# Attention and MLP block on one core: the first five units take their softmax denominators through one ones-matmul, the first statistics move partly to ScalarE, and queries run three units ahead

## Chip, cores and metric

One core of a Trainium2 chip. The metric is device microseconds of one execution of the program; lower is better. The kernel before was run three times: 1280.09, 1280.42 and 1280.76 us, so its median is 1280.42 us.

## What is computed

The reference, cut to what matters (`_layernorm` has eps 1e-5, `_B_ref` is an MLP block with two gelu layers on the same normed tokens):

```python
def _A_ref(x, k_cache, v_cache, wq, wo):          # x: 2048 x 512, 32 heads of 128, 2048 keys
    q = (x @ wq).reshape(B, Sq, H, Dh).transpose(0, 2, 1, 3)
    p = softmax(einsum("bhqd,bhkd->bhqk", q, k_cache) * Dh ** -0.5)
    o = einsum("bhqk,bhkd->bhqd", p, v_cache)
    return o.transpose(0, 2, 1, 3).reshape(B, Sq, H * Dh) @ wo

x = A_x
xn = _layernorm(x)
s = _A_ref(xn, A_k_cache, A_v_cache, A_wq, A_wo)
g = silu(_B_ref(xn, B_w1, B_w2, B_w3, B_w4))
return x + s * g
```

All inputs are bf16. The kernel subtracts no maximum in the softmax; the denominator is the sum over keys of exp(scores).

## The kernel before

**Units and slots.** The attention is cut into 128 units. A unit is one head and 512 queries (L121: eight groups of four heads; in a group the four blocks of 512 queries in turn, and in each block its four heads). A unit has eight slots (`SPU`, L54), each for two chunks of 128 keys. The main loop (L695) runs over all 1024 slots n; u is the unit, p the slot in it. In a slot TensorE makes two score matmuls into a two-bank PSUM tile `ps_s` (`s_slot`, L183), ScalarE takes exp of the 128x1024 tile into `pT` (L194), and TensorE makes the two value matmuls of five slots earlier into `ps_o` (`pv_slot`, L213, `LAG`, L55). `ps_s`, `ps_o` have two buffers each, `pT` four (two slots in each), and the two tags of the pool `psX`, "xa" and "xm", one bank each.

**Denominators.** VectorE adds the unit's four `pT` tiles: `add_first` at p = 4 (L200), `add_next` at p = 6 (L205), `add_last` at p = 0 of the next unit (L205, then a fold of 1024 columns, L210, and of 512, L211). That leaves for each query 128 partial sums, one on each partition. `sums` (L223), at p = 3 of the next unit, turns them into sums with four matmuls of one column each; the 512 sums then lie as 128 partitions x 4. `recip` (L231) inverts them (L233) and writes them to DRAM (`dr<-rc`, L235); `bcast` (L248), at p = 4, reads them back to all 128 partitions (`rb<-dr`, L250). `norm` (L253), at p = 2 of the second unit after, multiplies `ps_o` by `rb` into `oT` (L261).

**Queries.** `q_mm` (L167) makes a unit's 512 queries with four matmuls, `q_copy` (L175) casts them to `qT` (L180 on VectorE). Unit 0 has its own start (`first_tokens`, L377). Queries of units 1 to 3 are made in unit 0, those of unit 4 at the end of unit 2, and from unit 3 on those of unit u + 2 at p = 0 and 1 of unit u (L701 to L714).

**Layer norm.** 16 tiles of 128 tokens. A tile is loaded (L343), VectorE takes its statistics (L349, L350), GpSimd makes 1/sqrt(var + eps) of them in two small instructions (`rsqrt`, L116: L118, L119), VectorE applies mean and factor (L354), and the result is turned: for tiles 0 to 3 by TensorE against an identity (L386 to L400), for all others by a DMA transpose on SP's queue into `xnT` (L370). The first four tiles come ahead of the loop (L643 to L658); for the others a list of slots, `tokens` (L661), says when statistics, application and transpose are put into the queues.

**Order.** Every instruction of the path is pinned in program order, so each engine works through the order in which the code issues it, and what is issued after slot n by `at(n, ...)` stands behind that slot's own work in its engine's queue. Keys come by DMA transposes on SP's queue (`load_k`, L141), values by plain DMAs (`load_v`, L150, on SP too); for the heads of the first group their places are L649 to L673. SP's and GpSimd's DMAs pass eight completion semaphores in turn.

**MLP.** Its 136 chunks of four to five matmuls are spread over the slots p = 2, 3, 6 and 7 of units 5 to 119 (L638, L746); the output projections `wo_mm` (L266) fill p = 4 and 5 from unit 5 on. Until unit 5 there is nothing of either.

Of the kernel before, what the change touches and what calls it, by code (L numbers as in the profile page):

```python
# [8 lines left out]
ACT = mybir.ActivationFunctionType  # L9
ALU = mybir.AluOpType  # L10
# [7 lines left out]
def kernel(  # L18
# [40 lines left out]
    SHIFT = [1, -1, 2, -2]  # L59
    PADW = 8  # L60
    WARM = 48
    PSUM = bass.MemoryType.PSUM
    pin = tc.keep_in_program_order

    def pool(name, bufs=1, space=None, **kw):
# [9 lines left out]
    nhalf = const.tile([P, 1], FP32, name="nhalf")  # L75
    mv2 = const.tile([P, NT, nc.vector.BN_AGGR_DIM], FP32, name="mv2")
    rstd2 = const.tile([P, NT], FP32, name="rstd2")
    nc.vector.memset(ones_t[:], 1.0)
    nc.vector.memset(nhalf[:], -0.5)
    ident = const.tile([P, P], BF16, name="ident")  # L80
    diag = const.tile([P, P], FP32, name="diag")
# [1 line left out]
                       allow_small_or_imprecise_dtypes=True))  # L83
    pin(nc.vector.tensor_scalar(
        out=ident[:], in0=diag[:], scalar1=0.0, scalar2=None, op0=ALU.is_equal))

    kp = ent(pool("kp", HG + 1))
    vp = ent(pool("vp", HG + 1))
# [24 lines left out]
    def mm(out, lhsT, rhs, start, stop):  # L113
        pin(nc.tensor.matmul(out=out, lhsT=lhsT, rhs=rhs, start=start, stop=stop))  # L114

    def rsqrt(out, var):  # L116
        ve = smp.tile([P, 1], FP32, name="ve")
        pin(nc.gpsimd.tensor_scalar(out=ve[:], in0=var, scalar1=EPS, scalar2=None, op0=ALU.add))  # L118
        pin(nc.gpsimd.tensor_tensor(out=out, in0=ve[:], in1=nhalf[:], op=ALU.pow))  # L119

    units = [(g, qt, hh) for g in range(NG) for qt in range(QT) for hh in range(HG)]  # L121
    NU = len(units)
# [7 lines left out]
    def at(n, fn):  # L130
        todo[n].append(fn)
# [18 lines left out]
    def load_v(h, halves):  # L150
        v = A_v_cache[0, h].rearrange("(i p j) d -> p i j d", p=P, j=KJ)
        for i in halves:
            if i == 0:
                vBs[h] = vp.tile([P, KC, Dh], BF16, name="vb")
            ks = slice(i * KSPLIT // 2, (i + 1) * KSPLIT // 2)
            pin(nc.sync.dma_start(
                out=vBs[h].rearrange("p (i j) d -> p i j d", j=KJ)[:, ks], in_=v[:, ks]))

    def load_w(h, eng=nc.sync):
# [7 lines left out]
    def q_mm(u, dcs):  # L167
        g, qt, hh = units[u]
        if dcs[0] == 0:
            st[u] = dict(psq=psX.tile([P, 512], FP32, tag="xm" if u == HG else "xa", name="ps_q"))  # L170
        for dc in dcs:
            mm(st[u]["psq"][:], wqs[g * HG + hh][:, dc, :],
               xnT[:, dc, qt * 512:(qt + 1) * 512], dc == 0, dc == DC - 1)

    def q_copy(u):  # L175
        qT = qtp.tile([P, 512], BF16, name="qT")
        if u > QUIET + 1:
            pin(nc.scalar.activation(out=qT[:], in_=st[u].pop("psq")[:], func=ACT.Identity))
        else:
            pin(nc.vector.tensor_copy(out=qT[:], in_=st[u].pop("psq")[:]))  # L180
        st[u]["qT"] = qT
# [31 lines left out]
    def pv_slot(u, p):  # L213
# [5 lines left out]
        for j in range(2):  # L219
            kc = 2 * p + j  # L220
            mm(s["o"][:], vBs[g * HG + hh][:, kc, :], pT[:, 2 * (p % 2) + j, :], kc == 0, kc == KC - 1)

    def sums(u):  # L223
        s = st[u]
        ps = psX.tile([P, 4], FP32, tag="xa" if u + 1 < QUIET else "xm", name="ps_sum")
        a = s["acc"][:, 0, :].rearrange("k (p j) -> k j p", j=4)
        for j in range(4):
            mm(ps[:, j:j + 1], a[:, j, :], ones_t[:], True, True)
        recip(s, ps)

    def recip(s, ps):  # L231
# [5 lines left out]
    def split_sums(u, parts):  # L237
        s = st[u]
        if "ps" not in s:
            s["ps"] = psX.tile([P, 4], FP32, tag="xm", name="ps_sum")  # L240
        for a, first, last in parts:
            a = a.rearrange("k (p j) -> k j p", j=4)
            for j in range(4):
                mm(s["ps"][:, j:j + 1], a[:, j, :], ones_t[:], first and j == 0, last and j == 3)
        if parts[-1][2]:
            recip(s, s["ps"])

# [89 lines left out]


    ln = {}

    def ln1_load(t, eng):
        xin = tokp.tile([P, D], BF16, tag="ta", bufs=8, name="xin")
# [3 lines left out]
    def ln1_stats(t):  # L346
        xin = ln[t]
        bn = smp.tile([P, nc.vector.BN_STATS_DIM], FP32, name="bn")
        pin(nc.vector.bn_stats(out=bn[:], in_=xin[:]))  # L349
        pin(nc.vector.bn_aggr(out=mv1[t][:], in_=bn[:]))  # L350
        rsqrt(rs1[t][:], mv1[t][:, 1:2])

    def norm1(t, out, in_):
        pin(nc.vector.tensor_scalar(  # L354
# [3 lines left out]
    def ln1_norm(t):  # L358
        xin = ln.pop(t)
        xn = tokp.tile([P, D], BF16, tag="tb", bufs=8, name="xn")  # L360
        norm1(t, xn[:], xin[:])
        return xn
# [12 lines left out]
            mm(wt[:, 0, 0:P], ident[:], ident[:], True, True)  # L375

    def first_tokens():  # L377
        xns = [ln1_norm(t) for t in range(4)]
        st[0] = {}
        qA = psX.tile([P, 512], FP32, tag="xa", name="ps_q")  # L380
        qB = psX.tile([P, 512], FP32, tag="xm", name="ps_q")
        qT = qtp.tile([P, 512], BF16, name="qT")
        st[0]["qT"] = qT
        tps = []

        def turn(t):  # L386
            if t < 2:
                tp = psO.tile([P, DC, P], FP32, tag="ps_o", name="ps_o")[:]
            else:
                tp = psS.tile([P, 2, 512], FP32, name="ps_s")[:, 0, :].rearrange("p (c q) -> p c q", c=DC)  # L390
            for dc in range(DC):
                mm(tp[:, dc, :], xns[t][:, dc * P:(dc + 1) * P], ident[:], True, True)
            tps.append(tp)

        def back(t):
            dst = xnT[:, :, t * P:(t + 1) * P]
            if t == 2:
                pin(nc.vector.tensor_copy(out=dst, in_=tps[t]))
            else:
                pin(nc.scalar.activation(out=dst, in_=tps[t], func=ACT.Identity))  # L400

        def q_part(t):
# [12 lines left out]
        pin(nc.vector.tensor_copy(out=qT[:, 3 * P:], in_=qB[:, 3 * P:]))  # L415
# [49 lines left out]
    mv1 = [ph1.tile([P, nc.vector.BN_AGGR_DIM], FP32, name=f"mv1_{t}") for t in range(NT)]  # L465
    rs1 = [ph1.tile([P, 1], FP32, name=f"rs1_{t}") for t in range(NT)]

    def ph1_load():
        pin(nc.sync.dma_start(out=w1_sb[:], in_=B_w1.rearrange("(dc p) j -> p dc j", p=P)))
# [176 lines left out]
    pin(nc.scalar.activation(out=act1[:], in_=nhalf[:], func=ACT.Identity))  # L646
# [6 lines left out]
    for t in range(4):  # L653
        ln1_stats(t)
# [5 lines left out]
    load_k(2, (0, 1))  # L660
    tokens = ((2, 4, 5), (5, 9, 12), (8, 12, 13), (11, 14, 14),  # L661
              (21, 27, 27), (23, 29, 29), (29, 35, 35), (35, 39, 39),
              (39, 45, 45), (47, 53, 53), (55, 61, 61), (63, 69, 69))
    for t, (stats, apply, turn) in enumerate(tokens, 4):
        if t >= 8:
            at(stats - 8, lambda t=t: ln1_load(t, nc.gpsimd))
# [23 lines left out]
    for t in range(4 * LQ, NT):  # L690
        if t % 4 < 2:
            at((QUIET + 1 + 2 * (t % 4)) * SPU + 4, lambda t=t: gate_sum(t))

    wo_todo = deque()
    for n in range(NS):  # L695
        u, p = divmod(n, SPU)
# [1 line left out]
        m = n - LAG  # L698
        if m >= 0:
            pv_slot(*divmod(m, SPU))  # L700
        if u == 0 and p in (1, 3, 5):  # L701
            q_mm(1 + p // 2, range(DC))
        if u == 0 and p in (2, 4, 6):
            q_copy(p // 2)
        if u == HG - 2 and p in (6, 7):
            q_mm(HG, (2 * p - 12, 2 * p - 11))
        if u == HG - 2 and p == 7:
            q_copy(HG)
# [4 lines left out]
        if p == 2 and HG - 1 <= u < NU - 2:  # L713
            q_copy(u + 2)  # L714
        if p == 2 and u >= 2:
            norm(u - 2)
            gg, qq, hh = units[u - 2]
# [121 lines left out]
```

## Time and profile before

| what | value |
|---|---|
| runs | 1280.09, 1280.42, 1280.76 us |
| the profiled execution, its own time | 1279.53 us |
| its span, first to last instruction | 1277.8 us |
| TensorE matmul / ScalarE / VectorE busy | 98% / 87% / 80% |
| granted TensorE clock | 0.999 |
| matmuls, VectorE instructions | 6195, 1407 |
| DMA traffic | 111.79 MB, mean 87 GB/s |

How to read it: the profile is of one execution. A line such as `L205 DVE TENSOR_TENSOR` is the instruction of that line of the program, PE is TensorE, PEld its weight load, DVE VectorE, ACT ScalarE, POOL GpSimd, SP SyncE; a q behind the name is the engine's queue of issues. "<-" is read "made from" in a tile name and "released by" behind an idle time. Matmul rows overlap one another, so a busy TensorE row can be longer than the time that the matmul adds. The timeline gives start and duration of every instruction; the difference between the starts of two neighbours on a busy engine is what the first one costs in the queue.

### The profile page before, as it was taken

The numbers are of one execution on the slowest core, as the hardware profiler recorded it, in microseconds if no ns is written. First come the engines' busy times: TensorE is split into PE (matmuls) and PEld (weight loads), VectorE is DVE, ScalarE is ACT, GpSimd is POOL, SyncE is SP. The second block draws the span as 40 slices with busy tenths as digits, with TensorE's granted clock in tenths as the row PEclk, the third lists the DMA queues.
The fourth block names the chain that finished last, engine by engine and source line by source line (L and its number), as shares of the span: only waits on it lengthen the run. The fifth ranks groups of instructions, "written<-read, shape, count | busy, mean of one in ns | idle before, by whom it ended". The sixth has DMA issues, their size and how long they took to land.

```text
span 1277.8 us, 17233 instructions
## 1 busy us (share of the span) xinstructions
PE 1257.1 (98%) x6195; PEld 612.1 (48%) x6320; DVE 1019.2 (80%) x1407; ACT 1113.0 (87%) x1195; POOL 137.9 (11%) x241
## 2 busy tenths in 40 slices
PE   8999999999999999999999999999999999999998
PEld 5444444444444444444444444444444444444444
DVE  7888889898788877778887778887777888777886
ACT  7899998888999988899988889998888999888883
POOL 4430003323110010000001000000000000000110
PEclk9999999999999999999999999999999999999999
DMA  9644343455532564134443244523435133542532
GB/s 185 133 106 81 59 79 88 108 124 123 115 77 67 100 110 89 42 75 83 89 93 68 58 85 93 96 42 75 96 80 90 34 70 72 91 105 46 140 76 58
DMA packets 172950, 111.79 MB, mean 87 GB/s; under 512 B 124800, under 2 KB 149888, under 8 KB 172864
## 3 DMA queue, kind: packets, MB, share of 16 engines
q1 hardware_dynamic: 163904, 85.51, 34.3%
q0 software_dynamic: 8672, 24.91, 7.9%
q8 instruction: 49, 0.80, 0.3%
q14 instruction: 37, 0.30, 0.1%
q10 hardware_dynamic: 288, 0.26, 0.1%
HBM read 82.58 MB, written 7.60 MB: 71 GB/s over the span
## 4 chain that ended last, share of the span: by engine, by line
PE 87%; ACT 6%; DVE 4%; issue 1%; DMA 1%; POOL 0%; DVEq 0%; ACTq 0%
PE ps_s L114 31%; PE ps_o L114 30%; PE ps_m L114 9%; PE ps_wo L114 8%; PE ps_q L114 7%; ACT pT L194 4%; PE ps_sum L114 1%; ACT sq L425 1%; DVE acc L205 1%; ACT pre L455 1%; DVE bn L349 0%; DMA rb<-dr 0%; DMA xnT<-xn 0%; DVE acc L210 0%; DVE qT L180 0%
## 5 line engine op out<-in xcount | busy, mean ns | idle before, releaser
L194 ACT ACTIVATE pT<-ps_s 128x1024 bf16<-128x1024 f32 x1024 | 1012.0, 1031 | 141.0 <-PE ps_s L114 130.0
L114 PE MATMUL ps_s<-qT,kT 128*128 128x512 bf16 x2004 | 599.5, 379 | 4.1 <-ACT pT L194 1.0
L114 PE MATMUL ps_o<-pT,vb 128*128 128x512 bf16 x1997 | 597.6, 379 | 2.8
L205 DVE TENSOR_TENSOR acc<-acc,pT 128x2048 bf16<-128x2048 bf16 x254 | 309.8, 1220 | 65.5 <-ACT pT L194 60.8
L114 PEld LDWEIGHTS <-kT 128*128 128x128 bf16 x2048 | 226.8, 113 | 224.4 <-issue 18.6
L114 PEld LDWEIGHTS <-vb 128*128 128x128 bf16 x2048 | 199.8, 98 | 225.2
L200 DVE TENSOR_TENSOR acc<-pT 128x2048 bf16<-128x2048 bf16 x128 | 155.9, 1218 | 26.6 <-ACT pT L194 26.4
L114 PE MATMUL ps_q<-xnT,wq_h 128*128 128x512 bf16 (+1 forms) x519 | 150.7, 374 | 3.3 <-DMA xnT<-xn 2.0
L114 PE MATMUL ps_wo<-wo_h,oT 128*128 128x512 bf16 x456 | 136.3, 379 | 0.6
L328 DVE TENSOR_TENSOR s_acc<-ps_wo,s_acc 128x512 f32<-128x512 f32 x100 | 68.9, 689 | 73.9 <-PE ps_wo L114 71.0
L210 DVE TENSOR_TENSOR acc<-acc 128x1024 bf16<-128x1024 bf16 x127 | 87.9, 692 | 4.4
L261 DVE TENSOR_TENSOR oT<-ps_o,rb 128x512 bf16<-128x512 f32 x129 | 87.1, 676 | 4.1 <-DMA rb<-dr 4.0
L180 DVE CAST qT<-ps_q 128x512 bf16<-128x512 f32 x122 | 83.5, 685 | 4.8 <-PE ps_q L114 4.8
L114 PEld LDWEIGHTS <-wq_h 128*128 128x128 bf16 x524 | 50.6, 98 | 63.2 <-issue 3.6
L114 PEld LDWEIGHTS <-oT 128*128 128x128 bf16 x480 | 46.9, 98 | 57.7 <-issue 2.6
L114 PE MATMUL ps_m<-xn2T,w_sb 128*128 128x512 bf16 x222 | 66.1, 378 | 0.2
L114 PE MATMUL ps_m<-w_sb,h2T 128*128 128x512 bf16 x218 | 62.7, 379 | 0.2
L577 POOL DMA_DIRECT2D w_sb<-in_B_w_dram x28 | 21.1, 756 | 353.8 <-PE ps_m L114 328.6
L211 DVE TENSOR_TENSOR acc<-acc 128x512 bf16<-128x512 bf16 x127 | 54.0, 425 | 4.3
L233 DVE RECIPROCAL rc<-ps_sum 128x4 f32<-128x4 f32 x128 | 22.9, 179 | 40.9 <-PE ps_sum L114 40.0
L114 PEld LDWEIGHTS <-acc 128*128 128x128 bf16 x516 | 37.6, 115 | 29.6 <-issue 1.5
L609 POOL DMA_DIRECT2D g_d<-xr x16 | 8.8, 547 | 346.3 <-DVE xr L607 346.3
(74 smaller groups left out, 599.9 us busy)
## 6 DMA issues: line engine op xcount, KB each, us to landing
rb<-dr SPq DMA_DIRECT2D x128, 256.0 KB, 4.1
vb<-in_A_v_cache_dram SPq DMA_DIRECT2D x64, 256.0 KB, 4.5
w_sb<-in_B_w_dram POOLq DMA_DIRECT2D x28, 256.0 KB, 4.6
wo_h<-in_A_wo_dram SPq DMA_DIRECT2D x32, 128.0 KB, 3.9
wq_h<-in_A_wq_dram SPq DMA_DIRECT2D x28, 128.0 KB, 4.2
kT<-in_A_k_cache_dram SPq DMA_TRANSPOSE x128, 4.7
dr<-rc SPq DMA_DIRECT2D x128, 2.0 KB, 1.4
xr<-in_A_x_dram POOLq DMA_DIRECT2D x16, 128.0 KB, 3.5
```

Source lines behind the costliest of these rows:

```text
L114: pin(nc.tensor.matmul(out=out, lhsT=lhsT, rhs=rhs, start=start, stop=stop))
L180: pin(nc.vector.tensor_copy(out=qT[:], in_=st[u].pop("psq")[:]))
L194: pin(nc.scalar.activation(out=s["pT"][-1][:, jj:jj + 2, :], in_=sps[:], func=ACT.Exp, scale=SCALE))
L200: pin(nc.vector.tensor_tensor(out=s["acc"][:], in0=s["pT"][0][:], in1=s["pT"][1][:], op=ALU.add))
L205: pin(nc.vector.tensor_tensor(out=a[:], in0=a[:], in1=st[u]["pT"][i][:], op=ALU.add))
L210: pin(nc.vector.tensor_tensor(out=a[:, 0:2, :], in0=a[:, 0:2, :], in1=a[:, 2:4, :], op=ALU.add))
L211: pin(nc.vector.tensor_tensor(out=a[:, 0, :], in0=a[:, 0, :], in1=a[:, 1, :], op=ALU.add))
L233: pin(nc.vector.reciprocal(out=rc[:], in_=ps[:]))
L261: pin(nc.vector.tensor_tensor(out=oTs[(g, qt)][:, hh, c], in0=s["o"][:, c], in1=s["rb"][:, c], op=ALU.mult))
L328: pin(nc.vector.tensor_tensor(out=sa, in0=ps[:], in1=sa, op=ALU.add))
L425: pin(nc.scalar.activation(out=sq[:], in_=pre[:], func=ACT.Square, scale=GELU_A ** 0.5))
L577: pin(nc.gpsimd.dma_start(out=w[:], in_=w3_v[:, :, fc * P:(fc + 2) * P]))
```

## The change

It touches the first units and what runs ahead of them; from unit 6 on only the lead of the queries differs.

1. **Denominators of units 0 to 4** (`ONCHIP` = 5): `ones_t` becomes 128x128, and `sums_here` makes one matmul of 512 columns with the ones as weights, so each partition gets all 512 sums. VectorE inverts them from PSUM, 128x512, straight into `rb`. The four one-column matmuls, `dr<-rc` and `rb<-dr` of these five units go.
2. **First statistics:** tiles 0 and 2 stay on VectorE; tiles 1 and 3 take two passes of ScalarE each (`Identity` and `Square`, both with an accumulated sum), and a small VectorE instruction makes the mean. GpSimd makes the four factors in three pairs of instructions.
3. **Queries:** from unit 2 on those of unit u + 3 are made in unit u; those of unit 4 at slots 14 and 15 (`first_q`).
4. **Places:** the statistics, applications and transposes of tiles 4 to 7 move from slots 2 to 14 into slots 3 to 8; pieces 1 to 3 of the keys of head 2, until now issued ahead of the loop and at slots 2 and 4, come at slots 9 to 11, those of head 3 at 14 to 17, and the values of heads 2 and 3 go to GpSimd's queue.

```diff
+    ONCHIP = HG + 1
+    QL = 3
-    ones_t = const.tile([P, 1], BF16, name="ones_t")
+    ones_t = const.tile([P, P], BF16, name="ones_t")
...
     def q_mm(u, dcs):
-            st[u] = dict(psq=psX.tile([P, 512], FP32, tag="xm" if u == HG else "xa", name="ps_q"))
+            st[u] = dict(psq=psX.tile([P, 512], FP32, tag="xm" if u >= QUIET + QL else "xa", name="ps_q"))
...
+    def sums_here(u):
+        s = st[u]
+        ps = psX.tile([P, 512], FP32, tag="xm" if u + 1 < ONCHIP else "xa", name="ps_sum")
+        mm(ps[:], ones_t[:], s["acc"][:, 0, :], True, True)
+        s["rb"] = rp.tile([P, 512], FP32, name="rb")
+        pin(nc.vector.reciprocal(out=s["rb"][:], in_=ps[:]))
...
     def sums(u):
-        ps = psX.tile([P, 4], FP32, tag="xa" if u + 1 < QUIET else "xm", name="ps_sum")
+        ps = psX.tile([P, 4], FP32, tag="xa", name="ps_sum")
...
+    def first_stats():
...
+        def act(t):
+            pin(nc.scalar.activation(
+                out=junk[t][:], in_=ln[t][:], func=ACT.Identity, scale=-root / D, accum_out=nm[t][:]))
+            pin(nc.scalar.activation(
+                out=junk[t][:], in_=ln[t][:], func=ACT.Square, scale=root, bias=nm[t][:],
+                accum_out=mvA[:, t, 1:2]))
...
+        dve(0)
+        act(1)
+        dve(2)
+        act(3)
+        root_of(0, 1)
+        root_of(1, 3)
+        root_of(3, 4)
...
-    tokens = ((2, 4, 5), (5, 9, 12), (8, 12, 13), (11, 14, 14),
-              (21, 27, 27), (23, 29, 29), (29, 35, 35), (35, 39, 39),
+    tokens = ((3, 4, 5), (4, 5, 6), (5, 6, 7), (6, 7, 8),
+              (19, 23, 23), (21, 25, 25), (25, 29, 29), (29, 33, 33),
               (39, 45, 45), (47, 53, 53), (55, 61, 61), (63, 69, 69))
...
-    for n, h, piece in ((2, 2, 2), (4, 2, 3), (12, 3, 0), (15, 3, 1), (17, 3, 2), (20, 3, 3)):
+    for n, h, piece in ((9, 2, 1), (10, 2, 2), (11, 2, 3), (14, 3, 0), (15, 3, 1), (16, 3, 2), (17, 3, 3)):
         at(n, lambda h=h, piece=piece: load_k(h, (piece,)))
-    for n, h, half in ((7, 2, 0), (13, 2, 1), (20, 3, 0), (21, 3, 1)):
-        at(n, lambda h=h, half=half: load_v(h, (half,)))
+    for n, h, half in ((10, 2, 0), (11, 2, 1), (20, 3, 0), (22, 3, 1)):
+        at(n, lambda h=h, half=half: load_v(h, (half,), nc.gpsimd))
...
+    first_q = {1: (1, range(DC)), 3: (2, range(DC)), 5: (3, range(DC)),
+               14: (4, (0, 1)), 15: (4, (2, 3))}
+    first_copy = {2: 1, 4: 2, 6: 3, 15: 4}
...
-        if p in (0, 1) and HG - 1 <= u < NU - 2:
-            q_mm(u + 2, (2 * p, 2 * p + 1))
+        if p in (0, 1) and 2 <= u < NU - QL:
+            q_mm(u + QL, (2 * p, 2 * p + 1))
...
-            sums(u - 1)
-        if p == 4 and u >= 1:
+            (sums_here if u - 1 < ONCHIP else sums)(u - 1)
+        if p == 4 and u > ONCHIP:
             bcast(u - 1)
```

The applications of tiles 1 and 3 take their mean from the small VectorE instruction put ahead of them (`mean_of` in `first_tokens`). In VectorE's queue of the changed program, after statistics 4 and the cast of unit 2's queries, the order is: `add_first(0)`, apply 4, statistics 5, apply 5, statistics 6, cast of unit 3's queries, `add_next(0)`, apply 6, statistics 7, apply 7, `add_last(0)`, reciprocal 0.

More of the change, by code (lines that the diff above doesn't have):

```diff
@@ L73 @@
     s_acc = const.tile([P, NT, D], FP32, name="s_acc")
-    ones_t = const.tile([P, 1], BF16, name="ones_t")
-    nhalf = const.tile([P, 1], FP32, name="nhalf")
+    ones_t = const.tile([P, P], BF16, name="ones_t")
+    nhalf = const.tile([P, 2], FP32, name="nhalf")
     mv2 = const.tile([P, NT, nc.vector.BN_AGGR_DIM], FP32, name="mv2")
     rstd2 = const.tile([P, NT], FP32, name="rstd2")
-    nc.vector.memset(ones_t[:], 1.0)
     nc.vector.memset(nhalf[:], -0.5)
@@ L85 @@
         out=ident[:], in0=diag[:], scalar1=0.0, scalar2=None, op0=ALU.is_equal))
+    pin(nc.vector.memset(ones_t[:], 1.0))
     kp = ent(pool("kp", HG + 1))
@@ L118, in rsqrt @@
         pin(nc.gpsimd.tensor_scalar(out=ve[:], in0=var, scalar1=EPS, scalar2=None, op0=ALU.add))
-        pin(nc.gpsimd.tensor_tensor(out=out, in0=ve[:], in1=nhalf[:], op=ALU.pow))
+        pin(nc.gpsimd.tensor_tensor(out=out, in0=ve[:], in1=nhalf[:, 0:1], op=ALU.pow))
     units = [(g, qt, hh) for g in range(NG) for qt in range(QT) for hh in range(HG)]
@@ L148, in load_k, with load_v @@
                 in_=A_k_cache[0, h, i * w:(i + 1) * w, :], transpose=True))
-    def load_v(h, halves):
+    def load_v(h, halves, eng=nc.sync):
         v = A_v_cache[0, h].rearrange("(i p j) d -> p i j d", p=P, j=KJ)
@@ L155, in load_v @@
             ks = slice(i * KSPLIT // 2, (i + 1) * KSPLIT // 2)
-            pin(nc.sync.dma_start(
+            pin(eng.dma_start(
                 out=vBs[h].rearrange("p (i j) d -> p i j d", j=KJ)[:, ks], in_=v[:, ks]))
@@ L176, in q_copy @@
         qT = qtp.tile([P, 512], BF16, name="qT")
-        if u > QUIET + 1:
+        if u >= QUIET + QL:
             pin(nc.scalar.activation(out=qT[:], in_=st[u].pop("psq")[:], func=ACT.Identity))
@@ L221, in pv_slot @@
             mm(s["o"][:], vBs[g * HG + hh][:, kc, :], pT[:, 2 * (p % 2) + j, :], kc == 0, kc == KC - 1)
+    def sums_here(u):
[4 more added lines that the diff above has]
+        pin(nc.vector.reciprocal(out=s["rb"][:], in_=ps[:]))
     def sums(u):
         s = st[u]
[L225 removed]
+        ps = psX.tile([P, 4], FP32, tag="xa", name="ps_sum")
         a = s["acc"][:, 0, :].rearrange("k (p j) -> k j p", j=4)
         for j in range(4):
[L228 removed]
+            mm(ps[:, j:j + 1], a[:, j, :], ones_t[:, 0:1], True, True)
         recip(s, ps)
@@ L243, in split_sums @@
             for j in range(4):
-                mm(s["ps"][:, j:j + 1], a[:, j, :], ones_t[:], first and j == 0, last and j == 3)
+                mm(s["ps"][:, j:j + 1], a[:, j, :], ones_t[:, 0:1], first and j == 0, last and j == 3)
         if parts[-1][2]:
@@ L339 @@
     ln = {}
+    mvA = const.tile([P, 4, nc.vector.BN_AGGR_DIM], FP32, name="mvA")
+    rsA = const.tile([P, 4], FP32, name="rsA")
     def ln1_load(t, eng):
@@ L351, in ln1_stats, with dve, mean, root_of @@
         rsqrt(rs1[t][:], mv1[t][:, 1:2])
+    def first_stats():
+        root = D ** -0.5
+        nm = {t: smp.tile([P, 1], FP32, name="nm") for t in (1, 3)}
+        junk = {t: gtp.tile([P, D], BF16, tag="pre", name="pre") for t in (1, 3)}
+        def act(t):
[4 more added lines that the diff above has]
+                accum_out=mvA[:, t, 1:2]))
+        def dve(t):
+            bn = smp.tile([P, nc.vector.BN_STATS_DIM], FP32, name="bn")
+            pin(nc.vector.bn_stats(out=bn[:], in_=ln[t][:]))
+            pin(nc.vector.bn_aggr(out=mvA[:, t, :], in_=bn[:]))
+        def mean(t):
+            pin(nc.vector.tensor_scalar(
+                out=mvA[:, t, 0:1], in0=nm[t][:], scalar1=-1.0 / root, scalar2=None, op0=ALU.mult))
+        def root_of(a, b):
+            ve = smp.tile([P, b - a], FP32, name="ve")
+            pin(nc.gpsimd.tensor_scalar(
+                out=ve[:], in0=mvA[:, a:b, 1], scalar1=EPS, scalar2=None, op0=ALU.add))
+            pin(nc.gpsimd.tensor_tensor(
+                out=rsA[:, a:b], in0=ve[:], in1=nhalf[:, 0:b - a], op=ALU.pow))
+        dve(0)
[5 more added lines that the diff above has]
+        root_of(3, 4)
+        return mean
     def norm1(t, out, in_):
@@ L377, in first_tokens @@
     def first_tokens():
-        xns = [ln1_norm(t) for t in range(4)]
+        xns = []
+        for t in range(4):
+            if t % 2:
+                mean_of(t)
+            xns.append(ln1_norm(t))
         st[0] = {}
@@ L464 @@
     hT = ph1.tile([P, DC, Sq + PADW], BF16, name="hT")
-    mv1 = [ph1.tile([P, nc.vector.BN_AGGR_DIM], FP32, name=f"mv1_{t}") for t in range(NT)]
-    rs1 = [ph1.tile([P, 1], FP32, name=f"rs1_{t}") for t in range(NT)]
+    mv1 = [mvA[:, t, :] for t in range(4)]
+    mv1 += [ph1.tile([P, nc.vector.BN_AGGR_DIM], FP32, name=f"mv1_{t}") for t in range(4, NT)]
+    rs1 = [rsA[:, t:t + 1] for t in range(4)]
+    rs1 += [ph1.tile([P, 1], FP32, name=f"rs1_{t}") for t in range(4, NT)]
     def ph1_load():
@@ L645 @@
     act1 = const.tile([P, 1], FP32, name="act1")
-    pin(nc.scalar.activation(out=act1[:], in_=nhalf[:], func=ACT.Identity))
+    pin(nc.scalar.activation(out=act1[:], in_=nhalf[:, 0:1], func=ACT.Identity))
     for h in range(HG - 1):
@@ L652 @@
     warm_up(WARM)
-    for t in range(4):
-        ln1_stats(t)
+    mean_of = first_stats()
     load_w(HG - 1, nc.gpsimd)
@@ L659 @@
     load_v(1, (0, 1))
-    load_k(2, (0, 1))
-    tokens = ((2, 4, 5), (5, 9, 12), (8, 12, 13), (11, 14, 14),
-              (21, 27, 27), (23, 29, 29), (29, 35, 35), (35, 39, 39),
+    load_k(2, (0,))
+    tokens = ((3, 4, 5), (4, 5, 6), (5, 6, 7), (6, 7, 8),
+              (19, 23, 23), (21, 25, 25), (25, 29, 29), (29, 33, 33),
               (39, 45, 45), (47, 53, 53), (55, 61, 61), (63, 69, 69))
@@ L665 @@
         if t >= 8:
-            at(stats - 8, lambda t=t: ln1_load(t, nc.gpsimd))
+            at(stats - 6, lambda t=t: ln1_load(t, nc.gpsimd))
         at(stats, lambda t=t: ln1_stats(t))
@@ L700 @@
             pv_slot(*divmod(m, SPU))
[L701 to L708, printed above, removed]
-        if p in (0, 1) and HG - 1 <= u < NU - 2:
-            q_mm(u + 2, (2 * p, 2 * p + 1))
+        if n in first_q:
+            q_mm(*first_q[n])
+        if n in first_copy:
+            q_copy(first_copy[n])
+        if p in (0, 1) and 2 <= u < NU - QL:
+            q_mm(u + QL, (2 * p, 2 * p + 1))
         if p == 0 and u >= 1:
             add_last(u - 1)
-        if p == 2 and HG - 1 <= u < NU - 2:
-            q_copy(u + 2)
+        if p == 2 and 2 <= u < NU - QL:
+            q_copy(u + QL)
         if p == 2 and u >= 2:
```

## Prediction

> **What bounds the kernel now.** I read the page's shares first: TensorE's matmuls fill 98% of the span, and the chain that ended last is 87% TensorE. So for most of the span only fewer matmuls or less idle time would help, and the change takes away neither; it can only move time in the first units. The busy time by stretches of 10 us (columns: stretch, length, then busy us of TensorE, its weight load, VectorE, ScalarE, GpSimd, with counts) shows where TensorE isn't full:
>
> ```profile
> 10.00:20.00 10.00, 9.36 (x41) 4.43 (x43) 7.17 (x12) 8.61 (x10) 2.34 (x6) 1.00 1.19 249
> 20.00:30.00 10.00, 9.95 (x52) 4.86 (x52) 9.38 (x18) 10.00 (x12) 3.69 (x6) 1.00 0.62 132
> 30.00:40.00 10.00, 7.99 (x37) 3.68 (x37) 7.11 (x11) 6.87 (x9) 4.66 (x6) 1.00 0.86 141
> 40.00:50.00 10.00, 9.77 (x52) 4.74 (x52) 9.19 (x17) 9.32 (x11) 2.91 (x12) 1.00 0.79 173
> ...
> 80.00:90.00 10.00, 9.95 (x50) 4.91 (x50) 9.00 (x13) 9.46 (x12) 5.38 (x9) 1.00 0.72 200
> ```
>
> TensorE loses 0.64 us from 10 to 20 and 2.0 from 30 to 40, while VectorE runs at 9.4 and 9.2 of 10: early, VectorE has no room either. TensorE's waits from 30 to 60 us (total, times, longest) name what was lost:
>
> ```profile
> PE ps_q L114 <- DMA xnT<-xn: 2.0, 1, 2.0
> PE ps_sum L114 <- DVE qT L180: 0.6, 2, 0.4
> ```
>
> The first is the transpose of the next tokens: queries of unit 4 waited for `xnT`. The chain of waits in the same time (start, us, what) goes through VectorE's additions and the transfers:
>
> ```profile
> 17.95 1.14 DVE acc L205
> ...
> 19.18 1.24 DVE acc L205
> 20.44 0.70 DVE acc L210
> 21.16 0.43 DVE acc L211
> ...
> 28.84 0.69 DVE oT L261
> 29.54 4.31 DMA xnT<-xn
> ...
> 41.03 2.97 DMA dr<-rc
> 44.01 4.38 DMA rb<-dr
> ```
>
> The end of the fold (21.16 + 0.42) is where `sums` of unit 0 starts; its matmul stands in TensorE's queue, so nothing behind it starts earlier. In the timeline the sums of units 0 to 5 start at 21.78, 29.11, 40.37, 48.35, 57.39 and 67.66 us. I use these six marks: the change has done all it does by the last.
>
> **What a step costs.** Two neighbouring matmuls of 512 columns advance the chain by 0.43 us, so 0.2157 each. VectorE's steps, from start to next start in its timeline: addition of 2048 columns 1.14, or 1.26 if the next one uses its result (27.66 - 26.40); the folds 0.73 and 0.35, so `add_last` 2.34; query cast and `norm` 0.61 each; statistics 0.73 + 0.10; application 0.32. A step is about 0.09 shorter than the row's duration.
>
> **Part 2, the first statistics.** Now all four statistics run on VectorE before the first application (6.62), and GpSimd's fourth factor ends at 7.84, so the last application starts at 7.88. Afterwards ScalarE has tiles 1 and 3. A pass over 512 columns isn't in the trace with an accumulated sum; the row L604 (0.62 us, 512 columns from SBUF) is the nearest. From 3.6 (tile 1 landed, 3.57) four passes end at 6.2, the factor at 7.15, the application at 7.2: 0.7 us earlier. If each accumulation adds 0.2, nothing is won; the bound on the other side is GpSimd's three pairs one after another from 4.41, 0.87 each: 0.85. I take 0.6. The small mean instruction is under 0.2 and lies in GpSimd's time.
>
> **Part 4, the tokens in unit 0.** This is what I expect to cost first. An application right behind its own statistics waits for GpSimd, as the timeline of tile 6 shows:
>
> ```profile
> 22.23 0.18 DVE L350 BATCH_NORM_AGGREGATE mv<-bn 128x2 f32<-128x6 f32 x1
> ...
> 22.50 0.29 POOL L118 TENSOR_SCALAR ve<-mv 128x1 f32<-128x1 f32 x1 [4.16 <-DVE mv L350]
> ...
> 22.87 0.57 POOL L119 TENSOR_TENSOR rs<-ve,nhalf 128x1 f32<-128x1 f32 x1
> ```
>
> From the start of the aggregation to the factor's end it takes 23.44 - 22.23 = 1.2 us, where VectorE's step is 0.1. In the new order applications 5 and 7 stand right behind statistics 5 and 7: two bubbles of 1.1 us. Laid out: cast of unit 2's queries 13.8 (14.40 less 0.6), `add_first(0)` 14.4, application 4 at 15.6, statistics 5 15.9, bubble, application 5 17.8, statistics 6 18.1, cast 18.95, `add_next(0)` 19.55, application 6 20.7, statistics 7 21.0, bubble, application 7 22.9, `add_last(0)` 23.2 to 25.6. So sum 0 starts at **25.7 instead of 21.78**. Queued behind it on TensorE is slot 12, and ScalarE's exp behind that. Roughly, 2.2 of it are the bubbles and 2.6 the steps of tokens 6 and 7 that now stand ahead of the fold, less the 0.6.
>
> **Parts 1 and 3, denominators and queries, unit by unit.** Gone: four one-column matmuls (67.66 to 67.80: 0.14), a 0.09 step of VectorE, five `dr<-rc` and five `rb<-dr`. Their 0.32 to 0.34 us on SP's queue lie beside other work; their landing (2.97 + 4.38 in the chain) gave `norm` one wait of 0.46 us. New: one matmul of 0.22, and **a reciprocal of 128x512 from PSUM**. The trace has it only with four columns (mean ns after the busy time):
>
> ```profile
> L261 DVE TENSOR_TENSOR oT<-ps_o,rb 128x512 bf16<-128x512 f32 x127 | 86.4, 680 | 3.6 <-DMA rb<-dr 3.6
> L180 DVE CAST qT<-ps_q 128x512 bf16<-128x512 f32 x122 | 83.5, 685 | 4.8 <-PE ps_q L114 4.8
> ...
> L233 DVE RECIPROCAL rc<-ps_sum 128x4 f32<-128x4 f32 x128 | 22.9, 179 | 40.9 <-PE ps_sum L114 40.0
> ...
> L261 DVE TENSOR_TENSOR oT<-ps_o,rb 128x256 bf16<-128x256 f32 x2 | 0.8, 418 | 0.5 <-DMA rb<-dr 0.5
> ...
> L415 DVE CAST qT<-ps_q 128x128 bf16<-128x128 f32 x1 | 0.3, 290 | 1.0 <-PE ps_q L114 1.0
> ```
>
> The cast and `norm` give what a PSUM source costs: (685 - 290)/384 = 1.03 ns a column and 158 fixed, and (680 - 418)/256 = 1.02 and 156 fixed. Four columns would then take 160 ns, the reciprocal takes 179. If the 19 to 23 ns more belong to the four columns, one costs 5.2 to 5.8 ns, and 512 cost 2.8 to 3.1 us. If they are fixed, it's 0.69, as the cast; that is the lower bound, since no row of this shape is cheaper. With the longest row (184) and a fixed part of 150, it's 8.5 ns and 4.5 us, the upper. I take 3.1 (step 3.0), since a fixed extra would need a reason that no row gives.
>
> [...]
>
> VectorE between two sums, with the reciprocal behind cast and `norm`:
>
> - 0 to 1: wait for the sum 0.5, reciprocal 3.0, additions 1.26 + 1.14, cast 0.61, last 2.34: 8.86. TensorE needs 41 matmuls, 8.84.
> - 1 to 2: 1.22 + 3.0 + statistics 8, 9 1.66 + additions 2.28 + application 0.32 + 2.34 = 10.83 against 37 matmuls, 7.98.
> - 2 to 3: two applications and two statistics, second addition 1.26: 11.27 against 7.98.
> - 3 to 4: one of each, additions 1.26 + 1.14: 10.12 against 7.98.
> - 4 to 5: `ps_sum` of unit 4 takes the tag "xa", so unit 5's first `wo_mm` waits until the reciprocal is read: 1.22 + 3.0, and then 40 matmuls, 8.63: 12.83 together against 49 matmuls, 10.57.
>
> 25.7 + 8.86 + 10.83 + 11.27 + 10.12 + 12.83 = 79.6, **11.95 us later** than 67.66. ScalarE's exp waits with it: slot 0 of the next unit needs the buffer that `add_first` frees. The stall for `xnT` (2.0) goes, but VectorE is late there in any case. The same queries are made in all, one unit's four earlier, so 0.86 comes back at unit 125: **11.1 us**. After unit 6 nothing else differs. Pieces 1 to 3 of head 2's keys now stand on SP behind the transpose of tile 7 (23.3 + 1.2): the first leaves at 24.5, lands some 4 later (as the `kT` issues of that time do), and slot 18 needs it at about 33, so 4 us of cover; if sum 0 came at 21.2, that cover would be gone. The values on GpSimd's queue leave after the last factor (22.9), land by 29 and are needed at slot 21.
>
> The profiled execution took 1279.53; 1279.53 + 11.1 = 1290.6. The median of the runs is 0.9 above it: **1291.5 us**.
>
> **Rivals.**
> - *Dear reciprocal* (upper end, 4.5): each us of it counts five times, so 7.0 more, **1298.5**. For it: the longest rows. Against: the mean row. [...]
> - *Cheap reciprocal* (0.69, step 0.6): the intervals become 8.84, 8.42, 8.86, 7.98, 10.57, the mark 70.4, 2.7 late, less 0.86: **1282.3**. For it: the 20 ns may be fixed. It decides below about 1.5 us, where TensorE's 43.4 us equal VectorE's.
> - *Transfers, not VectorE, set units 0 to 5*, so the change wins: sum 0 at 21.2 and TensorE's own intervals (8.84, three of 7.98, 10.57) give 64.6, 3.1 early, with the 0.86 4.0: **1276.5**. For it: 29.54 to 33.85 and 41.03 to 48.39 in the chain are DMA. Against: VectorE's 9.4 of 10. It needs sum 0 by 22.4 and a reciprocal under 1.2 us.
>
> **Chances.** Forecast (reciprocal 2 to 3.9, 1286 to 1295.5) 0.62; dear 0.14; cheap 0.13; transfers 0.11. A measurement of this kernel tells about 0.2% (2.6 us) from no change. Faster: 0.11 and 0.02 of the cheap case, 0.13; same: 0.07 of the cheap case; slower: 0.80. The range leaves out the transfers, half of the cheap case's lower part and little of the dear one: **1281 to 1299**.
>
> **What would show it.** A row RECIPROCAL 128x512 of about 3.1 us, five times; `ps_sum` starts near 25.7, 34.6, 45.4, 56.7, 66.8 and 79.6; TensorE waiting some 4 us for `acc` before sum 0; VectorE idle 1 us for GpSimd ahead of applications 5 and 7; VectorE's second 40th of the span full. The forecast is wrong if the reciprocal is under 1.5 us, if sum 0 starts by 22.4, or if time is lost behind unit 6.

## The result and the profile after

| kernel | median (lowest to highest) | ratio to before [95% interval] |
|---|---|---|
| before | 1280.26 us (1280.05 to 1280.76) | |
| after | 1296.42 us (1295.59 to 1297.02) | 1.0125 [1.0108, 1.0143] |

The change costs 16.2 us; 11.1 were forecast. The profiled execution of after took 1297.02 us, 17.49 above that of before. Its groups by line show the new operation beside the old one (after the bar: busy us, mean ns of one):

```profile
L230 DVE RECIPROCAL rb<-ps_sum 128x512 f32<-128x512 f32 x5 | 16.8, 3351 | 1.1 <-PE ps_sum L116 1.1
...
L242 DVE RECIPROCAL rc<-ps_sum 128x4 f32<-128x4 f32 x123 | 22.0, 179 | 41.0 <-PE ps_sum L116 40.2
```

From the two rows a column costs (3351 - 179)/508 = 6.24 ns, with 154 ns fixed: the fixed part is that of the cast and `norm`, and the 20 ns more belong to the columns. Stretches of 10 us, as those shown of before:

```profile
20.00:30.00 10.00, 5.50 (x17) 2.00 (x16) 8.23 (x10) 4.11 (x5) 3.93 (x7) 0.72 0.64 133
30.00:40.00 10.00, 10.00 (x44) 4.60 (x43) 8.63 (x10) 7.96 (x9) 0.00 (x0) 0.93 0.42 77
40.00:50.00 10.00, 7.80 (x35) 3.42 (x33) 9.63 (x16) 6.97 (x8) 5.60 (x10) 1.00 0.45 93
...
70.00:80.00 10.00, 7.22 (x25) 2.95 (x25) 8.40 (x9) 3.77 (x5) 0.76 (x3) 0.83 0.12 27
```

From 40 to 50 VectorE is at 9.63 and TensorE has fallen to 7.80: VectorE bounds these units. The column behind the five engines is the granted clock: 0.72, 0.93 and 0.83 here, where before has 1.00 in these stretches. From 30 to 40 TensorE is "busy" for all of its 10 us, but the first 1.3 of them at half clock. TensorE's waits from 0 to 100 us:

```profile
PE ps_sum L116 <- DVE acc L213: 7.7, 3, 4.5
PE ps_wo L116 <- DVE rb L230: 2.2, 1, 2.2
...
PE ps_sum L116 <- DVE qT L182: 1.6, 1, 1.6
```

The 4.5 us stand ahead of sum 0, the 2.2 are unit 5's `wo_mm` behind the last reciprocal: both as forecast. The wait of before for `xnT` is gone. In VectorE's timeline the two bubbles ahead of applications 5 and 7:

```profile
18.46 0.41 DVE L402 TENSOR_SCALAR xn<-xin,mv,rs 128x512 bf16<-128x512 bf16 x1 [0.99 <-POOL rs L121]
...
23.53 0.41 DVE L402 TENSOR_SCALAR xn<-xin,mv,rs 128x512 bf16<-128x512 bf16 x1 [1.00 <-POOL rs L121]
```

**The clock.** In after's records of the granted clock it is 0.50 from 24.47 us for 6.83 and from 75.67 for 3.41. Both lengths are multiples of 3.413, and so are the distances of the two starts (51.20, 15 times) and from the first to the next half clock, at the end of the span (1294.23 us, 372 times). So I cut the traces into windows of 3.413 us on the grid of each run (that of before is counted back from its only half clock, at 1274.45 us). After, columns as before (length, TensorE busy first, clock behind POOL):

```profile
21.06:24.47 3.41, 0.76 (x4) 0.24 (x3) 2.38 (x6) 1.52 (x2) 1.76 (x4) 1.00 0.19 38
24.47:27.89 3.42, 1.57 (x4) 0.55 (x4) 2.68 (x4) 0.10 (x1) 1.60 (x3) 0.50 0.76 175
27.89:31.30 3.41, 3.41 (x9) 1.18 (x8) 3.41 (x2) 2.04 (x3) 0.00 (x0) 0.50 1.16 199
31.30:34.71 3.41, 3.41 (x17) 1.58 (x16) 2.52 (x4) 2.73 (x3) 0.00 (x0) 1.00 0.69 140
68.85:72.26 3.41, 1.80 (x8) 0.71 (x7) 3.38 (x5) 1.58 (x3) 1.58 (x2) 1.00 0.16 41
72.26:75.67 3.41, 1.22 (x6) 0.61 (x6) 3.41 (x3) 0.84 (x2) 0.00 (x0) 1.00 0.00 0
75.67:79.09 3.42, 3.42 (x10) 1.22 (x8) 2.31 (x4) 1.89 (x2) 0.00 (x0) 0.50 0.19 38
```

The windows with 0.76 and 1.22 us of matmuls are followed by half clock; that with 1.80 isn't. At half clock, the window with 1.57 was followed by a second one. Before has its wait for `xnT` in this window:

```profile
31.99:35.41 3.42, 1.41 (x7) 0.74 (x8) 1.23 (x2) 1.16 (x2) 2.26 (x3) 1.00 0.75 88
```

1.41 us of matmuls, and the clock stays. Up to 85 us, after has two full-clock windows with at most 0.37 of their length in matmuls (those above, 0.22 and 0.36) and before has none. Windows of three kernels below are as empty: 0.73 us of 3.413 (0.21) in that with part 4's places on before; 1.13 (0.33) in that with unit 4's queries later; 1.27 (0.37) in that with head 3's values on GpSimd's queue as well. All five were followed by half clock. No full-clock window of before or after with 0.41 or more was, up to 85 us, and neither was one of 1.45 us (0.42) in the kernel with the values on SyncE's queue. The 0.41 is the window of before above, in which the record of one matmul is missing (8 weight loads, 7 matmuls); with it, it is 0.43.

### The profile page after: what moved, and what is told of

Same layout as the page of the kernel before. It is cut to its first block, busy times and chain, and to the rows that moved or that the text cites. A ratio compares the mean times of both kernels' runs of the same rounds, so it can differ in the third digit from the quotient of the medians.

```text
span 1295.3 us, 17322 instructions
## 1 busy us (share of the span) xinstructions
PE 1270.6 (98%) x6305; PEld 614.1 (47%) x6305; DVE 1034.4 (80%) x1406; ACT 1115.7 (86%) x1202; POOL 138.1 (11%) x243
## 4 chain that ended last, share of the span: by engine, by line
PE 88%; ACT 6%; DVE 4%; DMA 1%; issue 0%; POOL 0%; DVEq 0%; ACTq 0%; SPq 0%
PE ps_s L116 32%; PE ps_o L116 30%; PE ps_m L116 9%; PE ps_wo L116 8%; PE ps_q L116 7%; ACT pT L196 4%; PE ps_sum L116 1%; ACT sq L477 1%; DVE rb L230 1%; DVE acc L207 1%; ACT pre L507 1%; DMA xin<-in_A_x_dram 1%; DVE bn L360 0%; DVE acc L202 0%; DVE acc L212 0%
## 5 line engine op out<-in xcount | busy, mean ns | idle before, releaser
L116 PE MATMUL ps_s<-qT,kT 128*128 128x512 bf16 x2048 | 610.6, 380 | 3.7 <-ACT pT L196 2.4
L116 PE MATMUL ps_o<-pT,vb 128*128 128x512 bf16 x2048 | 610.3, 380 | 0.6 <-DVE oT L270 0.6
L116 PE MATMUL ps_wo<-wo_h,oT 128*128 128x512 bf16 x468 | 139.3, 380 | 2.2 <-DVE rb L230 2.2
```

## The experiments

Each ratio is to runs of before on the same chip, and where two kernels are compared, it's by what each costs above these runs. Six kernels are after with one thing changed, six are before with something added or moved.

**Reciprocal made a copy.** The inversion of the first five units' denominators is left out.

```diff
-        pin(nc.vector.reciprocal(out=s["rb"][:], in_=ps[:]))
+        pin(nc.vector.tensor_copy(out=s["rb"][:], in_=ps[:]))
```

> The reciprocal of the first five units is replaced by a copy of the same 128x512 from PSUM; the inversion of these denominators is left out. VectorE-queue theory: the row costs 0.69 instead of 3.35 us, the stall ahead of sum 0 and the half clock behind it stay (sum 0 at 26.3, sum 1 at about 37.7), then the intervals fall to about 8.4, 8.9, 8.0 and 10.6 instead of 10.6, 11.4, 10.9 and 14.4, so sum 5 near 73.6 instead of 85.0 and the time near 1286 us. Rival (the stall at sum 0 and what the clock does behind it carry the loss, and the reciprocal lies beside them): at most 3 us less than the changed kernel, about 1294.

Measured: 1284.9 us, 1.0037 [1.0022, 1.0052]; the row of the copy:

```profile
L230 DVE COPY rb<-ps_sum 128x512 f32<-128x512 f32 x5 | 3.4, 687 | 1.2 <-PE ps_sum L116 1.1
```

Five times (3351 - 687) is 13.3 us; what is left of the 16.2 is 5.3, so 10.9 went. The interval from sum 1 to 2 fell from 10.58 to 8.07 and that from 4 to 5 from 14.39 to 10.36. So the reciprocal's length sets these intervals, and the dear instruction, not the on-chip scheme, is the larger part of the loss.

**The bubbles taken out** by one slot more between statistics and application:

```diff
-    tokens = ((3, 4, 5), (4, 5, 6), (5, 6, 7), (6, 7, 8),
+    tokens = ((3, 4, 5), (4, 6, 7), (5, 7, 8), (6, 8, 9),
```

> Applications 5 to 7 stand one slot later, so that none is right behind its own statistics. VectorE-queue theory: the two bubbles of 1.0 us go and application 7 moves behind the fold (0.3), so sum 0 starts near 24.0 instead of 26.3; TensorE's wait there is 2.2 instead of 4.5 us, too short for the clock to drop, and the interval from sum 0 to sum 1 falls from 11.4 to about 9.5: 4 us less, about 1292. Rival (the order of the tokens is paid anyway, since the transposes of the tokens now come later for the queries of unit 4): no gain, 1296.

Measured: 1295.14 us, 1.0121 [1.01, 1.0142], a miss for my theory. That 2.2 us are too short for the clock to drop was an estimate from before, where a wait of 1.96 us left it at 1.00; here TensorE's waits for the additions are 1.8 us at the longest, and it is 1.00 up to 28.79. Sum 0 came at 23.32 instead of 26.32 (0.5 of it because a load of tokens landed earlier), but TensorE's waits say where the 3 us went:

```profile
PE ps_q L116 <- DMA xnT<-xn: 2.6, 1, 2.6
```

The first queries of unit 4 now wait for the last transpose, the clock is halved in its turn (0.50 from 28.79 us for 3.41), and sum 1 is only 1.05 us earlier at 36.64. The bubbles stood in front of a second limit.

**TensorE kept busy** while it waits for sum 0, with 72 matmuls of 128 columns into the sum's own bank, overwritten by the sum:

```diff
+        if u == 0:
+            for _ in range(72):
+                mm(ps[:, 0:P], ident[:], ident[:], True, True)
```

> Adds 72 matmuls of 128 columns into the same PSUM tile ahead of sum 0, about 4 us of work in a stall of 4.5 us. Theory that the half clock costs time of its own: granted clock 1.00 from 20 to 40 us, sum 0 unmoved near 26.3, sum 1 2 to 2.5 us earlier than 37.7, the time about 1294. Rival (VectorE's queue sets the pace anyway, the clock costs nothing): the clock recovers, the time stays at 1296.

Measured: 1294.89 us, 1.0119 [1.0104, 1.0134]. The granted clock stays 1.00 up to the last matmuls. The real sum 0 comes at 25.85, and the interval to sum 1 is 10.28 instead of 11.37; that from 4 to 5 is 12.71 instead of 14.39, with the clock at 1.00 from 70 to 80 us, where after has 0.83. So the half clock cost 1.1 us over two windows and 1.7 over one; 0.6 of it is lost again at slot 72, where a wait shown further on is longer here (the lag of ScalarE's exp, by how much it starts later than in before, grows by 2.0 instead of 1.37). What is left between sums 0 and 1 is read from the chain of that kernel:

```profile
26.27 3.36 DVE rb L233
29.62 1.09 DVE acc L202
...
30.81 1.23 DVE acc L207
32.03 0.61 DVE qT L182
...
32.69 0.59 PE ps_q L116 x2
...
36.30 0.23 PE ps_sum L116
```

The chain leaves VectorE at the query cast: unit 3's queries are behind it in TensorE's queue, and 3.6 us of matmuls stand from there to sum 1. My sum let them run beside VectorE's fold (34.52 + 0.42 there).

**Denominators through DRAM again**, all else as after:

```diff
-    ONCHIP = HG + 1
+    ONCHIP = 0
```

> All denominators go through DRAM as in the kernel before; the first statistics, the token order and the query lead stay changed. VectorE-queue theory: sum 0 stays at 26.3 and sum 1 near 37.7, then TensorE's own intervals of 8.0, 8.0, 8.0 and 10.6, sum 5 near 72 and the time near 1285, so two thirds of the loss are the reciprocals and one third is the token order. Rival (the removed DRAM trips are worth something once the reciprocal is paid): slower than the copy variant by more than 1 us, since it waits for rb<-dr.

Measured: 1286.02 us, 1.0046 [1.0031, 1.0061]. Parts 2 to 4 without part 1 cost 6.4, so part 1 is 9.8 of the 16.2 (sum 0 at 25.89, half clock from 24.77 for 6.83).

**Part 1 alone, on before** (the diff's `sums_here`, `ones_t` and `ONCHIP = 5`; all five sums stand in the bank "xa" of the queries, where after has only sum 4):

> The kernel before with part 1 alone: ones-matmul and reciprocal from PSUM for units 0 to 4, all else as before. VectorE-queue theory: sum 0 stays at 21.8 with no wait for it, then VectorE's own steps with 3.35 us for the reciprocal give intervals of about 9.9, 10.9, 11.2, 10.9 and 12.8, sum 5 near 77.5 instead of 67.7: about 10 us more than before, 1289.5. Rival (the new token order, which fills VectorE's queue ahead of sum 0, is needed for the reciprocal to hurt): under 5 us more.

Measured: 1290.24 us, 1.0088 [1.0074, 1.0102], 10.6 more than before. 10.6 and 6.4 make 17.0, against 16.2: within 0.8 us the parts add up, so none pays for another. The trace is of the slowest of its four executions (1293.37 us; the others took 1290.02 to 1290.32) and misses what I expected of it in two places: sum 0 is at 23.45 instead of 21.78, since tile 4's load landed 2 us later, and the last two intervals are 11.95 and 14.48 instead of 10.9 and 12.8. There sum 4 waits for a cast of queries in its bank, and the clock is halved from 68.19 us for 6.83; how much each takes isn't worked out.

**Four units on chip instead of five:**

```diff
-    ONCHIP = HG + 1
+    ONCHIP = HG
```

> The changed kernel with four units on chip instead of five, so unit 4's sums no longer hold the bank that unit 5's first output projection needs. Theory: the wait of 2.2 us for rb, the reciprocal's 3.3 us and the half clock behind the wait go from the last interval: 14.4 becomes 10.5 to 11, the time about 1292.5. Rival (the last interval is VectorE's queue alone): 14.4 falls by no more than the 1.3 us by which VectorE's own steps exceed TensorE's, about 1295.

Measured: 1292.35 us, 1.01 [1.0085, 1.0116]. The interval from sum 4 to 5 is 10.27, that of before, where after has 14.39. By this the fifth unit alone costs 4.1 us, more than its reciprocal: TensorE stands behind it, and then runs at half clock. By the medians it is 3.4.

**Tile 15 turned three slots earlier.** After loses 1.2 us at 111 us, which I had not forecast. Its waits from 85 to 130 us name a transfer of denominators:

```profile
PE ps_q L116 <- DMA rb<-dr: 1.2, 1, 1.2
```

But tile 15's transpose is issued behind that one on SP's queue, and queries that are made three units ahead need it at slot 72.

```diff
-              (39, 45, 45), (47, 53, 53), (55, 61, 61), (63, 69, 69))
+              (39, 45, 45), (47, 53, 53), (55, 61, 61), (60, 66, 66))
```

> The kernel after with the last token's places at slots 60, 66, 66 instead of 63, 69, 69, so that tile 15's transpose is issued three slots earlier. My theory (the queries of unit 12, made three units ahead at slot 72, wait for that transpose): TensorE's 1.2 us idle at 111-112 us goes, the lag no longer steps from 17.32 to 18.69 us between units 8 and 9, and the time is some 1.2 us less than after, about 1295.2 us. Rival: what is waited for is the transfer of the denominators that the profile names there; then the step stays and the time is that of after, 1296.4 us.

Measured: 1294.51 us, 1.0118 [1.0104, 1.0132]; after's interval overlaps, so the time alone doesn't settle it. The trace does: TensorE has no wait from 85 to 130 us, and ScalarE's exp runs 16.22 us behind before's in units 8 and 9, where after goes from 17.32 to 18.69. The wait was for the transpose; the profile named the other transfer. In after's trace too, that transfer had landed at 111.47, the transpose landed at 112.13 and the queries went on at 112.22. The profiled executions differ by 2.44 us: 1.37 are this, 0.76 the first half-clock stretch (one window here, whose interval of 10.61 is 0.33 above that with the 72 matmuls, and two in after), and 0.35 an earlier sum 0.

**Parts 4 and 2 on before.** The values of heads 2 and 3 on GpSimd's queue, piece 0 of head 3's keys from slot 12 to 15 and piece 1 to 16, so that SyncE issues the transposes of the tokens earlier; in a second kernel the first statistics on ScalarE too.

```diff
-    for n, h, piece in ((2, 2, 2), (4, 2, 3), (12, 3, 0), (15, 3, 1), (17, 3, 2), (20, 3, 3)):
+    for n, h, piece in ((2, 2, 2), (4, 2, 3), (15, 3, 0), (16, 3, 1), (17, 3, 2), (20, 3, 3)):
...
-        at(n, lambda h=h, half=half: load_v(h, (half,)))
+        at(n, lambda h=h, half=half: load_v(h, (half,), nc.gpsimd))
```

> The kernel before with only two places changed: values of heads 2 and 3 on GpSimd's queue, and the first key piece of head 3 behind the transpose of tile 7. Theory (in the kernel before the wait of 2.0 us for xnT is SP's queue, where tile 7's transpose stands behind a value load and a key piece): the transposes of tiles 6 and 7 leave 1 to 2.5 us earlier, the wait goes, 1.5 to 2 us less than before: ratio about 0.9986. Rival (the wait only hides VectorE's queue, which then ends last): the interval from sum 1 to sum 2 falls by under 0.7 us, no gain that can be measured.

> b1 with the first statistics on ScalarE as well (part 2). Theory: the first exp comes 0.1 to 0.4 us earlier, as in the changed kernel and its variants, and some of it arrives at sum 0, where TensorE waited 0.2 us for VectorE: ratio 0.0002 under b1's, not to be told from b1. Rival (ScalarE's four passes pay as meant): 0.6 us or more under b1.

Measured: 1283.28 us, 1.003 [1.0018, 1.0042], and 1283.8 us, 1.0033 [1.002, 1.0045]: a miss, and part 2 brings nothing. Tile 7's transpose was issued at 27.14 instead of 29.54 and landed at 35.93 instead of 33.85: 8.8 us under way instead of 4.3. Two halves of the values, two token loads and the 256 KB of `rb<-dr` were in flight when it was issued or right after; that they slowed it is argued here, and the next kernels bear it out. TensorE's wait for it doubled, and the clock was halved behind it (from 36.70 us for 3.41):

```profile
PE ps_q L114 <- DMA xnT<-xn: 4.0, 1, 4.0
```

**Unit 4's queries later, on before**, so that the wait for `xnT` can go. Two follow-ups move the values of head 3 as well, to slots 18 and 19 on GpSimd's or on SyncE's queue.

```diff
-        if u == HG - 2 and p in (6, 7):
-            q_mm(HG, (2 * p - 12, 2 * p - 11))
-        if u == HG - 2 and p == 7:
+        if u == HG - 1 and p in (2, 3):
+            q_mm(HG, (2 * p - 4, 2 * p - 3))
+        if u == HG - 1 and p == 4:
```

> The kernel before with the queries of unit 4 moved from unit 2's slots 6 and 7 to unit 3's slots 2 and 3; nothing of the change is in it. My theory: the wait of TensorE for the transposed inputs (1.96 us in before) goes, since the transposes land before those queries are due; the interval from sum 1 to sum 2 falls from 11.25 to 7.4-7.7 us, that from sum 2 to sum 3 rises from 7.98 to some 8.84 us, and the time is 2.5 to 3 us less than before, some 1277 us (ratio 0.998). Rival: VectorE's queue or the keys of head 3 end last at the same place anyway; then the interval stays above 10 us and the gain is under 0.7 us.

> The late-queries kernel (the kernel before with unit 4's queries in unit 3), and with it the values of head 3 issued on GpSimd's queue at slots 18 and 19 instead of SyncE's at 20 and 21. My theory: what took the gain back was the values' place behind the denominators' two transfers on SyncE's queue (issued 36.73, landed behind them), so issued some 5 us earlier they land before they are needed at 39.6 us; the 2.8 us wait for vb goes, the interval from sum 2 to 3 falls from 12.31 to 8.8 us, and the time is some 2.3 us less than before, about 1277.5 us (ratio 0.998). Rival: the DMA engines are the limit, as when the values of heads 2 and 3 both went to GpSimd's queue; then the values take their time from the keys or the denominators, another wait takes the place and the time is that of before or more.

> As the kernel that is sent with it, but the values of head 3 stay on SyncE's queue, at slots 18 and 19, that is ahead of the two transfers of unit 1's denominators. My theory: the same gain, some 2.3 us less than before, if the place in the order and not the queue decides; the denominators leave 1.1 us later, and the normalization of unit 1, which waited 3.4 us for them in the late-queries kernel, waits some 1 us longer without holding up TensorE. Rival: the later denominators hold up the normalization, VectorE's additions behind it and so the next sum; then sum 3 is not earlier than 48.4 us and the time is that of before or more.

Measured: 1282.09 us, 1.0013 [1.0004, 1.0022]; 1280.02 us, 1.0007 [0.9998, 1.0016]; 1282.23 us, 1.0018 [1.0009, 1.0027]. Three misses, and the waits of TensorE from 20 to 75 us tell why. The first kernel, then the values on GpSimd's queue, then on SyncE's:

```profile
PE ps_o L114 <- DMA vb<-in_A_v_cache_dram: 2.8, 1, 2.8
```

```profile
PE ps_q L114 <- DVE acc L210: 2.1, 1, 2.1
```

```profile
PE ps_o L114 <- DVE oT L261: 3.3, 1, 3.3
```

In the first the interval from sum 1 to 2 did fall to 8.90, and then the values of head 3 landed late and the next one was 12.31 instead of 7.98. The clock was also halved behind the wait, from 41.87 us for 3.41, in the profiled execution. Of the eleven the three with a mean granted clock of 0.999 or more took 1279.52 to 1280.16 us, as long as before, and the eight with 0.998, the profiled one among them, 1281.61 to 1282.49. That this depends on where the windows fall is my estimate, not shown. In the second the values came in time, but tile 7's transpose, issued at 29.77, landed at 35.92, and at 36.05 the queries went on (the profile names VectorE's fold, which ended at 35.93 and which the queries don't read). In the first the same transpose took 3.9 us; only the values' place differs, and with them beside it the transpose took 6.2. In the third `norm` waited 5.2 us for `rb<-dr`. In the three, another transfer of 30 to 42 us landed last each time, and TensorE waited. The clock takes part too. The windows of the second and the third kernel:

```profile
33.92:37.33 3.41, 1.27 (x6) 0.65 (x7) 2.41 (x4) 0.97 (x2) 3.30 (x13) 1.00 1.10 145
37.33:40.74 3.41, 3.41 (x9) 1.21 (x8) 0.69 (x1) 1.83 (x2) 0.01 (x1) 0.50 0.74 152
```

```profile
38.13:41.54 3.41, 1.45 (x11) 0.62 (x9) 0.00 (x0) 2.16 (x3) 0.00 (x0) 1.00 1.05 143
```

The wait of 2.1 us, which lies in one window, was followed by half clock (0.50); that of 3.3, which two windows share, left it at 1.00. No kernel tried here beats before.

## Why the prediction was right in the whole, and where it was off

Direction and mechanism held: VectorE, with a reciprocal of over 3 us in its queue, sets units 0 to 5. Of the rivals, *cheap reciprocal* and *transfers* are out by the row of 3351 ns; *dear* (4.5) is too high by 1.15. It is the row that tells these apart and not the time: 1296.42 lies above the bounds of my own case (1286 to 1295.5), though the reciprocal of 3.35 lies inside it (2 to 3.9), and it is nearer to the 1298.5 of *dear* than to 1291.5. That nearness is luck, made by the terms below. The sum ends 5.4 us apart at sum 5, step by step (us):

| step | forecast | measured | why |
|---|---|---|---|
| sum 0 | 25.7 | 26.32 | unit 2's cast at 14.53, not 13.8; from there 11.79 as forecast (11.9), with bubbles of 1.0, not 1.1 |
| sum 0 to 1 | 8.86 | 11.37 | reciprocal's step 3.27, not 3.0; half clock 1.1; TensorE's matmuls behind the cast 1.19 |
| 1 to 2 | 10.83 | 10.58 | |
| 2 to 3 | 11.27 | 11.42 | |
| 3 to 4 | 10.12 | 10.91 | sum 4 shares the bank "xa" with the queries and waited 0.6 for their cast; reciprocal 0.27 |
| 4 to 5 | 12.83 | 14.39 | half clock 1.7; `wo_mm` wait as forecast |

- **Reciprocal.** Value taken 3.1, measured 3.35. The choice between the readings of the 20 ns was right, and it carried the forecast; the error of 0.27 a step shows only four or five times.
- **Part 2.** The bound that I named and didn't take ("if each accumulation adds 0.2, nothing is won") is what happened: each pass has a row ACTIVATION_READ_ACCUMULATOR of 0.19 us behind it, passes start 0.74 apart, and the first exp came at 10.80 instead of 10.92. Even that doesn't reach sum 0: statistics 4, ahead of unit 2's cast in VectorE's queue, wait for tile 4's load, which the sum left out. After, and then before:

```profile
13.70 0.69 DVE L360 BATCH_NORM_STATS2 bn<-xin 128x6 f32<-128x512 bf16 x1 [0.92 <-DMA xin<-in_A_x_dram]
14.43 0.18 DVE L361 BATCH_NORM_AGGREGATE mv<-bn 128x2 f32<-128x6 f32 x1
14.53 0.66 DVE L182 CAST qT<-ps_q 128x512 bf16<-128x512 f32 x1
```

```profile
13.44 0.69 DVE L349 BATCH_NORM_STATS2 bn<-xin 128x6 f32<-128x512 bf16 x1 [0.53 <-DMA xin<-in_A_x_dram]
```

The load's landing varies: in four other kernels with this order of tokens (72 matmuls, DRAM, four units, tile 15) the cast is at 14.04 to 14.15 and sum 0 at 25.85 to 25.97, in that with the copy they are at 14.85 and 26.65. Alone part 2 was worth nothing in the pair of kernels on before.
- **Half clock.** I read the granted clock of before as 1.00 and carried it over, although I forecast TensorE waiting 4 us for sum 0. That is the step that failed: a wait was priced at its length, and here the clock was also halved for two windows after the first wait and for one after the second. It cost 1.1 + 1.7 = 2.8 us.
- **"Needed at" of a queue.** From sum 0 to 1 I compared VectorE's total with TensorE's total and took the larger. The chain changes engines at the cast, and its two halves add up: 1.19 missed.
- **"After unit 6 nothing else differs."** Wrong: queries three units ahead need tile 15's transpose eight slots sooner. It cost 1.37 us, which the tile's earlier place gave back. Time lost behind unit 6 was one of my own signs of a wrong forecast, and it did show. As forecast the lead pays at the end: the lag falls from 18.69 to 17.33 us, 1.36 where 0.86 was forecast. The two cancel, by luck.
- **The stall for `xnT`.** I had that it goes but brings nothing, since VectorE is late there. The kernels on before show a second reason: without it another transfer is late at the same place.

The terms: 0.6 at sum 0, 2.5, 0.8 and 1.6 in three intervals, 0.1 less in the other two, together 5.4; 11.95 + 5.4 = 17.3 at sum 5 and at the end. The profiled execution of after lies 0.60 above its median and that of before 0.73 below: 17.49 - 1.33 = 16.16, the difference of the medians.

## What to carry to other kernels

Before a transfer is replaced by work on an engine, price that work in the queue of the engine which is fullest in that stage; here 7.4 us of DMA beside other work went, and 3.3 us of VectorE's time on the path came in its place, five times. A stall of TensorE cost 0.3 to 1.7 us more than its own length here where the clock was halved behind it; look at matmul time window by window, and spread or fill a wait that can't be removed. When a stall on a transfer is to be moved away, ask what lands next on the same engines: four moves in a row only changed the name of the wait.

## What the runs showed of the hardware

- The clock fell to half after five windows of 3.413 us with 0.21 to 0.37 of their length in matmuls, and did not after those with 0.42 and 0.53; before's stall of 1.96 us, at 1.00, stood at 0.41 by its records, or 0.43 with the one that is missing, next to the edge.
- VectorE's reciprocal of 128x512 f32 from PSUM took 3351 ns, 4.9 times a copy of the same shape (687).
- Each ScalarE pass with an accumulated sum had an instruction of 0.19 us behind it; the passes of 512 columns started 0.74 us apart.
- A DMA transpose issued 2.4 us earlier landed 2.1 us later, with more loads in flight beside it; in two kernels that differ only in where two value loads are issued it took 3.9 and 6.2 us.
